# Second layer's wide blocks: the product with w_in by one level of Strassen's scheme over pairs of packets

## The chip, the cores and the metric

The kernel runs on one core of a Trainium2 chip. The metric is the device time of one execution in microseconds. A core has a matrix engine (TensorE, PE), whose weight loads are listed apart (PEld), and three engines for elementwise work: VectorE (DVE), ScalarE (ACT) and GpSimd (POOL). Each engine works through its own instructions in a fixed order, and instructions wait for each other across engines by semaphores. Data lie in SBUF, 128 partitions wide; matmuls write to PSUM, of which this kernel uses eight banks of 512 fp32 columns.

## The reference

Forgetting attention is followed by two MLPs. The second MLP, the only part that changes, is `_moe2_ref`; its x is the first MLP's output.

```python
def _moe2_ref(x, w_in, w_out, alpha):          # x 2304x512, w_in 512x2048, w_out 2048x512
    h = x @ w_in
    g = np.maximum(h, 0.0) + alpha * np.minimum(h, 0.0)
    return (g @ w_out).astype(np.float32)
```

## The kernel before, in words

The time axis has two layers of MLP blocks. Layer 0 works on blocks of 256 tokens while the attention of later tokens runs beside it on the other engines. Layer 1 is the second MLP: one narrow block of 256 tokens (t = 0) and four wide blocks of 512 tokens (`SIZES[1]`). The 2048 hidden units are cut into 16 packets of 128 (`NF`); a packet holds 128 columns of w_in and 128 rows of w_out.

Products have fp32 accuracy by splitting: `split` makes a high part (a cast by ScalarE to float32r) and a low part (the difference, by VectorE unless told otherwise) of each operand, and three matmuls, high by high, high by low and low by high, stand for one product. `packet(1, f)` keeps both parts of a packet's weights in SBUF for the whole of layer 1.

For one block, `mlp_block` returns `up`, `down` and `finish`. `up(f)` multiplies packet f's columns of w_in with the block's x: four chunks of 128 input features by three terms, 12 matmuls of 512 columns in one bank (L712). ScalarE makes the two relus of the result (L731, L735), VectorE joins them to the leaky relu `r` (L736), and `split` writes its high and low part into `ring`, a buffer for four packets. `down(f, g)` adds packet f's part of the output: four groups of 128 tokens by three terms, again 12 matmuls of 512 columns, in four banks that collect over all 16 packets (L758). `finish` scales the banks into `res` tiles and writes them out (L783, L785, L795). The main loop calls `up` three packets ahead of `down` (`LAG[1]` = 3), and `inputs` of the next block at f = 10.

`wide_inputs` loads x of a wide block from `x2_d` (an intermediate in DRAM), and splits it; the parts of consecutive blocks lie in two sets of tiles, so that a block's x is split while the one before is still in use. The order of each engine's instructions is made by a scheduler from the program's order and its own estimates; at run time it is fixed.

Of the kernel before, what the change touches and what calls it, by code (L numbers as in the profile page):

```python
# [19 lines left out]
def tile_forget_attention__then__two_mlps(  # L20
# [20 lines left out]
    nc = tc.nc  # L41
# [20 lines left out]
    REBASE, W_SCALE = 2.0**-111, 2.0**8  # L62
# [10 lines left out]
    ps = ctx.enter_context(tc.tile_pool(name="ps", bufs=2, space=PSUM))  # L73
# [11 lines left out]
    gate_s, gate_b, bsum, nalpha = misc[:, 0:1], misc[:, 1:2], misc[:, 4 : 4 + NCC], misc[:, 8 : 8 + NF]  # L85
# [167 lines left out]
    xf = {}  # L253
# [366 lines left out]
    x2_d = dram.tile([NB, P, NCC * T], F32, name="x2_d")  # L620


    SIZES = [[(t, 1) for t in range(NB - 2)] + [(NB - 2, 2)], [(0, 1)] + [(t, 2) for t in range(1, NB, 2)]]
    BLOCKS = [(layer, t) for layer in range(2) for t in range(len(SIZES[layer]))]

    def inputs(layer, t):

        first, count = SIZES[layer][t]
        if count == 2:
            return wide_inputs(layer, t, first)  # L630
# [16 lines left out]
        for c in range(NCC):  # L647
            on_pool = layer == 0 and t
            split(xh[c], xl[c], src[:, c], nc.gpsimd if on_pool else nc.vector)
        return xh, xl  # L650

    def wide_inputs(layer, t, first):
        xh, xl = [], []
        src = []
        for half in range(2):
            if layer == 1:
                src.append(xfp.tile([P, 2, 2, T], F32, tag="xf", name=f"x2_{t}_{half}"))
                for z in range(2):
                    nc.sync.dma_start(
                        out=src[half][:, :, z],  # L660
                        in_=x2_d[first + z, :, half * 2 * T : (half + 1) * 2 * T].rearrange("p (c n) -> p c n", n=T),
                    )
            for parts, tag, spare in ((xh, "xh", "raw"), (xl, "xl", "probs")):
                name = f"{tag}{layer}_{t}_{half}"
                if layer == 0:
                    if half:
                        part = two.tile([P, 1024], F32R, tag="raw", name=name)
                    else:
                        part = one.tile([P, 1024], F32R, tag=f"{tag}1", name=name)
                elif t % 2:  # L670
                    part = two.tile([P, 1088 if spare == "probs" else 1024], F32R, tag=spare, name=name)
# [15 lines left out]
    wide_ring = []  # L687

    def mlp_block(layer, t, x):


        xh, xl = x
        acc = acc_tiles(f"acc{layer}_{t}")
        banks = [a.rearrange("p a n -> p (a n)") for a in acc]
        first, count = SIZES[layer][t]
        TB = count * T
# [4 lines left out]
        def up(f):  # L701
# [37 lines left out]
            split(gh, gl, r, nc.gpsimd if layer == 0 and count == 1 else nc.vector)  # L739
            return gh, gl  # L740

        def down(f, g):
            w = packet(layer, f)
            if layer == 0:
                terms = ((w[2], g[0]), (w[3], g[0]), (w[2], g[1]))
                for d in range(NCC):
                    for n, (a, b) in enumerate(terms):
                        nc.tensor.matmul(  # L748
                            banks[d] if count == 2 else acc[d // 2][:, d % 2], a[:, d * P : (d + 1) * P], b,
                            start=(f == 0 and (d % 2 == 0 or count == 2) and n == 0),  # L750
                            stop=(f == NF - 1), skip_group_check=True,
                        )
            else:
                gh, gl = g
                _, _, woh, wol = w
                for m in range(TB // P):
                    for a, b in ((gh, woh), (gh, wol), (gl, woh)):
                        nc.tensor.matmul(  # L758
                            banks[m], a[:, m * P : (m + 1) * P], b,
                            start=(f == 0 and b is woh and a is gh), stop=(f == NF - 1 and a is gl),  # L760
                        )

        def finish():
            for m, bank in enumerate(banks):
                if m % 2 == 0:
                    pool = xfp if m else one
                    both = pool.tile([P, 1024], F32, tag="xf" if m else "res", name=f"res{layer}_{t}_{m}")
                res = both[:, m % 2 * 512 : (m % 2 + 1) * 512]
# [125 lines left out]
```

## Time and profile before

| what | value |
|---|---|
| time, median of 3 runs | 1048.67 us (1044.5 to 1049.79) |
| profiled execution, its own time | 1046.88 us |
| its span, first to last instruction | 1045.1 us |
| mean granted clock of TensorE | 0.996 of full speed |
| TensorE (PE) busy | 1030.9 us, 99% |
| ScalarE (ACT) busy | 625.7 us, 60% |
| VectorE (DVE) busy | 587.1 us, 56% |
| GpSimd (POOL) busy | 362.5 us, 35% |

The four wide blocks take the time from about 687 us to the end. A busy share is an average over the whole span; what an engine does in one stage is read from the table by stretches. Matmuls overlap in the pipeline, so the time from one start to the next, and not a matmul's duration, tells what it costs.

### The profile page before, as it was taken

What the parts mean: (1) busy time and instruction counts of PE and PEld (TensorE: products, weight loads), DVE (VectorE), ACT (ScalarE), POOL (GpSimd) and SP (SyncE); (2) the same over time, 40 slices, a digit from 0 to 9 for tenths busy, and PEclk for the clock granted to TensorE, in tenths of its full rate; (3) what the DMA queues carried; (4) which work ended last, traced back from release to release, by engine and by line L of the source; (5) the groups of instructions that cost most, each with busy time, mean ns of one, the idle gap of its engine ahead of it and who ended that gap; (6) DMA issues with size and microseconds to landing.
All of it is one profiled execution on the core that took longest, in us unless ns stands there. A gap on an engine that the chain in (4) does not pass through costs nothing.

```text
span 1045.1 us, 18431 instructions
## 1 busy us (share of the span) xinstructions
PE 1030.9 (99%) x6372; PEld 910.0 (87%) x6376; DVE 587.1 (56%) x1421; ACT 625.7 (60%) x1493; POOL 362.5 (35%) x768
## 2 busy tenths in 40 slices
PE   9899999999999999999999999999999999999998
PEld 4578899999999999999998888988888888888887
DVE  6979864787667775767665766532223224223222
ACT  5877876777778786878776766533234334333232
POOL 5656775666677566777550000000000000000000
PEclk9999999999999999999999999999999999999999
DMA  7988442343133341324115753200002002001001
GB/s 155 266 218 234 124 73 64 74 99 75 40 85 76 89 83 41 89 62 97 54 58 175 242 161 94 88 21 1 1 1 81 1 1 81 1 0 41 1 1 41
DMA packets 173470, 83.36 MB, mean 80 GB/s; under 512 B 135552, under 2 KB 160896, under 8 KB 173376
## 3 DMA queue, kind: packets, MB, share of 16 engines
q1 hardware_dynamic: 169296, 81.61, 29.8%
q10 hardware_dynamic: 4080, 0.57, 0.3%
q8 instruction: 50, 0.82, 0.3%
q14 instruction: 44, 0.36, 0.1%
HBM read 72.63 MB, written 9.51 MB: 79 GB/s over the span
## 4 chain that ended last, share of the span: by engine, by line
PE 85%; DMA 4%; ACT 3%; DVE 3%; POOL 2%; issue 1%; SPq 1%; ACTq 0%; DVEq 0%; POOLq 0%
PE hp L712 36%; PE acc L758 19%; PE acc L748 17%; PE av L527 4%; PE pt L511 4%; PE sc L456 2%; DMA wo<-in_moe_w_out_dram 2%; PE sc L455 1%; DMA vn<-in_v_dram 1%; DVE wt L142 1%; PE colsum L241 1%; PE sc L453 1%; DVE probs L431 1%; ACT probs L469 1%; SPq L332 1%
## 5 line engine op out<-in xcount | busy, mean ns | idle before, releaser
L712 PE MATMUL hp<-xh,w 128*128 128x256 f32 (+1 forms) x1536 | 396.5, 330 | 0.3 <-ACT r L731 0.3
L712 PEld LDWEIGHTS hp<-xh,w 128*128 128x128 f32 x1536 | 267.5, 189 | 26.9 <-ACT r L731 0.7
L712 PE MATMUL hp<-xl,w 128*128 128x256 f32 (+1 forms) x768 | 253.0, 329 | 0.0
L731 ACT ACTIVATE r<-hp 128x256 f32<-128x256 f32 (+1 forms) x208 | 96.3, 463 | 224.2 <-PE hp L712 214.9
L758 PE MATMUL acc<-w,ring 128*128 128x512 f32 x864 | 209.0, 390 | 0.0
L758 PEld LDWEIGHTS acc<-w,ring 128*128 128x128 f32 x864 | 161.3, 188 | 33.2
L748 PE MATMUL acc<-gh,w 128*128 128x256 f32 x896 | 172.3, 286 | 0.4 <-ACT res L774 0.3
L736 DVE SCALAR_TENSOR_TENSOR r<-u,misc,r 128x512 f32<-128x512 f32 (+1 forms) x80 | 55.8, 697 | 200.4 <-ACT u L735 200.4
L712 PEld LDWEIGHTS hp<-xl,w 128*128 128x128 f32 x768 | 145.2, 189 | 13.4 <-issue 0.4
L748 PEld LDWEIGHTS acc<-gh,w 128*128 128x128 f32 x896 | 136.0, 189 | 3.1 <-issue 1.6
L748 PE MATMUL acc<-gl,w 128*128 128x256 f32 x448 | 118.7, 288 | 1.8 <-POOL gl L131 1.8
L469 ACT ACTIVATE probs<-probs,nm 64x64 f32<-64x64 f32 (+4 forms) x160 | 90.0, 563 | 37.1 <-DVE nm L457 25.0
L480 POOL TENSOR_SCALAR probs<-probs,sm 64x64 f32<-64x64 f32 (+4 forms) x160 | 90.9, 581 | 60.5 <-DVE sm L477 49.9
L131 POOL TENSOR_TENSOR gl<-r,gh 128x256 fp32r<-128x256 f32 x112 | 89.5, 799 | 51.0 <-ACT gh L130 44.5
L131 DVE TENSOR_TENSOR ring<-r,ring 128x512 fp32r<-128x512 f32 (+1 forms) x96 | 62.1, 647 | 60.6 <-ACT ring L130 60.4
L457 DVE CUSTOM_DVE_ANT_0 probs<-sc,probs 128x320 f32<-128x320 f32 (+3 forms) x160 | 68.2, 427 | 41.0 <-PE sc L456 32.0
L130 ACT CAST ring<-r 128x512 fp32r<-128x512 f32 (+1 forms) x96 | 56.1, 584 | 53.3 <-DVE r L736 52.6
L748 PEld LDWEIGHTS acc<-gl,w 128*128 128x128 f32 x448 | 80.1, 188 | 4.6 <-POOL gl L131 2.5
L511 PE MATMUL pt<-ident,probs 128*128 128x128 f32 x480 | 74.4, 276 | 4.8 <-POOL probs L480 4.6
L545 DVE TENSOR_TENSOR xf<-av,xf 64x128 f32<-64x128 f32 (+3 forms) x88 | 28.0, 319 | 67.9 <-ACT xf L544 67.5
L511 PEld LDWEIGHTS pt<-ident,probs 128*128 128x128 f32 x480 | 54.7, 140 | 10.9 <-POOL probs L480 7.0
L431 DVE TENSOR_SCALAR probs<-cum,cumT 64x64 f32<-64x64 f32 (+4 forms) x137 | 62.5, 504 | 2.9 <-issue 0.9
(117 smaller groups left out, 1579.3 us busy)
## 6 DMA issues: line engine op xcount, KB each, us to landing
wi<-in_moe_w_in_dram SPq DMA_DIRECT2D x32, 512.0 KB, 4.9
wo<-in_moe_w_out_dram SPq DMA_DIRECT2D x32, 512.0 KB, 5.0
cum<-cum_d SPq DMA_DIRECT2D x32, 288.0 KB, 3.7
cum<-cum_d SPq DMA_DIRECT2D x30, 160.0 KB, 3.1
nat<-in_k_dram SPq DMA_DIRECT2D x64, 72.0 KB, 2.5
x_d<-res SPq DMA_DIRECT2D x18, 256.0 KB, 2.3
out_dram<-res SPq DMA_DIRECT2D x18, 256.0 KB, 2.1
vn<-in_v_dram SPq DMA_DIRECT2D x32, 128.0 KB, 2.8
```

The costliest lines, as they stand in the source:

```text
L130: nc.scalar.copy(hi, src)
L131: lo_eng.tensor_tensor(out=lo, in0=src, in1=hi.bitcast(F32), op=ALU.subtract)
L431: nc.vector.tensor_scalar(out=pt[:rows, :i1], in0=u.cums[h][:rows, :i1], scalar1=cumT[:rows, r, head : head + 1], scalar2=0.0, op0=ALU.sub ...
L457: nc.vector.tensor_tensor_reduce(out=pt[:rows, j0:j1], in0=scr, in1=pt[:rows, j0:j1], scale=SCALE if flip else -SCALE, scalar=init, op0=AL ...
L469: nc.scalar.activation(pt[:rows, :n], pt[:rows, :n], AF.Exp, bias=nm[:rows, m : m + 1], scale=1.0 if flip else -1.0, accum_out=sm[:rows, m ...
L480: nc.gpsimd.tensor_scalar(out=probs[r][:rows, :n], in0=probs[r][:rows, :n], scalar1=sm[:rows, m : m + 1], scalar2=1.0, op0=ALU.mult, op1=A ...
L511: nc.tensor.transpose(tp[:, o : o + P], u.probs[h][r][:, k0 : k0 + P], ident)
L712: nc.tensor.matmul(hs, a[:, c], b[c], start=(n == 0), stop=(n == len(terms) * NCC - 1))
L731: relus.append(nc.scalar.activation(r, hs, AF.Relu, scale=1.0 / W_SCALE).ins)
L736: nc.vector.scalar_tensor_tensor(out=r, in0=u, scalar=nalpha[:, f : f + 1], in1=r, op0=ALU.mult, op1=ALU.add)
L748: nc.tensor.matmul(banks[d] if count == 2 else acc[d // 2][:, d % 2], a[:, d * P : (d + 1) * P], b, start=(f == 0 and (d % 2 == 0 or count ...
L758: nc.tensor.matmul(banks[m], a[:, m * P : (m + 1) * P], b, start=(f == 0 and b is woh and a is gh), stop=(f == NF - 1 and a is gl),)
```

## The change

In the wide blocks of layer 1, two packets (256 hidden units) are taken together. Their weights form a matrix of 2 by 2 blocks: the packet (1 or 2) by the half of the input features (`halves`: chunks 0 and 1, or 2 and 3). The block's x forms another one: the half of the features by the half of the tokens (256 each). One level of Strassen's scheme (in the form of Winograd, which shares sums) replaces the eight block products by seven. Each product is six matmuls of 256 columns, two chunks by three terms.

- `strassen_inputs` replaces `wide_inputs` for layer 1. It loads x in two pieces, forms four differences (`t1` to `t4`) on VectorE and GpSimd, and splits seven operands, numbered by product in `OPERANDS`. The tiles are one set: the next block's operands are written into the same ones.
- `weight_sums(pair, which)` forms four sums of weight blocks from high and low parts: sums 1, 2 and 4 on GpSimd (three, two and two steps of 256 columns), sum 3 on VectorE (three steps), and splits them into `sums`, one tile of high and one of low parts. `next_sums` calls it a pair ahead.
- `up_first(f)`, for the first packet of a pair, issues products 1, 6 and 5 into banks a, b and c. ScalarE copies a and c to `t1` and `t5`, VectorE makes `u2` = b + `t1`. `up_second(f)` adds product 7 to b, 2 to a, 3 to c and 4 to b. Before 4, VectorE reads b for `u3`; after it, b for `cc`, of which GpSimd makes the second half from `u3` and `t5`. Two leaky relus (`relu_pair`, `prelu`) give both packets.
- `finish` of the wide blocks takes its `res` tiles from the tags `ph` and `pl`.

```diff
-    def wide_inputs(layer, t, first):
+    def strassen_inputs(t, first):
+        src = []
+        for j in range(2):
+            src.append(xfp.tile([P, 2, 2 * T], F32, tag="xf", name=f"x2_{t}_{j}"))
+            nc.sync.dma_start(out=src[j], in_=x2_d[first + j].rearrange("p (k n) -> p k n", k=2))
...
+        t3 = minus(room[:, : 2 * T], b22, b12, nc.gpsimd)
+        t1 = minus(b12, b12, b11, nc.vector)
+        t2 = minus(room[:, 2 * T :], b22, t1, nc.vector)
+        for c in range(2):
+            cols = slice(c * T, (c + 1) * T)
+            minus(t4[c], b21[:, cols], t2[:, cols], nc.gpsimd)
+        for n, x in ((1, b11), (6, t2), (5, t1), (7, t3), (2, b21), (3, b22)):
+            split(*parts[n], x)
...
+    def weight_sums(pair, which):
...
+        if 1 in which:
+            chain(nc.gpsimd, s[1], h2[:, 0], (add, h2[:, 1]), (add, l2[:, 0]), (add, l2[:, 1]))
+            chain(nc.gpsimd, s[2], s[1], (sub, h1[:, 0]), (sub, l1[:, 0]))
+            sums[2:] = [s[2]]
+        else:
+            chain(nc.vector, s[3], h1[:, 0], (sub, h2[:, 0]), (add, l1[:, 0]), (sub, l2[:, 0]))
+            chain(nc.gpsimd, s[4], h1[:, 1], (sub, sums[2]), (add, l1[:, 1]))
+        for n in which:
+            split(sums[0][:, n - 1], sums[1][:, n - 1], s[n])
...
+        def multiply(bank, n, a, start):
+            (ah, al), (bh, bl) = a, x[0][n]
+            for c in range(2):
+                for z, (lhs, rhs) in enumerate(((ah, bh), (ah, bl), (al, bh))):
+                    nc.tensor.matmul(
+                        bank, lhs[:, c * P : (c + 1) * P], rhs[:, c],
...
+        def up_first(f):
...
+            multiply(a, 1, left[1], True)
+            nc.scalar.copy(t1, a)
+            multiply(b, 6, left[6], True)
+            nc.vector.tensor_tensor(out=u2, in0=b, in1=t1, op=ALU.add)
+            multiply(c, 5, left[5], True)
+            nc.scalar.copy(t5, c)
...
+            next_sums(f, (1, 2))
+            return holder
+
+        def up_second(f):
...
+            multiply(b, 7, left[7], False)
+            nc.vector.tensor_tensor(out=u3, in0=b, in1=t1, op=ALU.add)
+            multiply(a, 2, left[2], False)
+            relu_pair(r[:, :T], u[:, :T], a)
+            multiply(c, 3, left[3], False)
+            nc.vector.tensor_tensor(out=u2, in0=c, in1=u2, op=ALU.add)
+            relu_pair(r[:, T:], u[:, T:], u2)
+            holder.extend(prelu(r, u, f - 1))
+            multiply(b, 4, left[4], False)
+            cc = one.tile([P, 512], F32, tag="vn", name=f"cc_{name}")
+            nc.gpsimd.tensor_tensor(out=cc[:, T:], in0=u3, in1=t5, op=ALU.add)
+            nc.vector.tensor_tensor(out=cc[:, :T], in0=b, in1=t1, op=ALU.add)
...
+            relu_pair(r, u, cc)
+            g = prelu(r, u, f)
+            next_sums(f, (3, 4))
+            return g
...
-        return up, down, finish
+        return up_strassen if layer == 1 and count == 2 else up, down, finish
```

How the order of instructions changes, on VectorE first, in the second wide block of layer 1 around packets 9 to 11. Before, a packet takes two instructions, the leaky relu (L736) and the low part for `ring` (L131):

```order
L736 SCALAR_TENSOR_TENSOR r_2_9_11302<-u_2_9_11303,misc,r_2_9_11302 128x512
L131 TENSOR_TENSOR ring_9986<-r_2_9_11302,ring_9982 128x512
L736 SCALAR_TENSOR_TENSOR r_2_10_11334<-u_2_10_11335,misc,r_2_10_11334 128x512
L131 TENSOR_TENSOR ring_9987<-r_2_10_11334,ring_9983 128x512
L736 SCALAR_TENSOR_TENSOR r_2_11_11384<-u_2_11_11385,misc,r_2_11_11384 128x512
L131 TENSOR_TENSOR ring_9988<-r_2_11_11384,ring_9984 128x512
```

After the change, at the same place, from the leaky relu of packet 9 (L812) to the first half of `cc` of packet 11. `sum_6_12123`, `sum_6_12227` and `sum_6_12228` are sums 1, 3 and 4 for packets 12 and 13, `sum_7_12346` is sum 3 for packets 14 and 15, `u_2_11` is `u3`, `u_2_10` is `u2`:

```order
L812 SCALAR_TENSOR_TENSOR ph_2_9_12066<-pl_2_9_12067,misc,ph_2_9_12066 128x512
L131 TENSOR_TENSOR sums_l<-sum_6_12123,sums_h 128x256
L131 TENSOR_TENSOR ring_9986<-ph_2_9_12066,ring_9982 128x512
L850 TENSOR_TENSOR u_2_11_12183<-p_2_10_12097,t_2_10_12099 128x256
L131 TENSOR_TENSOR sums_l<-sum_6_12227,sums_h 128x256
L854 TENSOR_TENSOR u_2_10_12101<-p_2_10_12098,u_2_10_12101 128x256
L812 SCALAR_TENSOR_TENSOR ph_2_11_12181<-pl_2_11_12182,misc,ph_2_11_12181 128x512
L131 TENSOR_TENSOR sums_l<-sum_6_12228,sums_h 128x256
L723 TENSOR_TENSOR sum_7_12346<-w_14_60_10032,w_15_16_10094 128x256
L131 TENSOR_TENSOR ring_9987<-ph_2_11_12181,ring_9983 128x512
L723 TENSOR_TENSOR sum_7_12346<-sum_7_12346,w_14_59_10033 128x256
L860 TENSOR_TENSOR cc_11_12217<-p_2_10_12097,t_2_10_12099 128x256
```

Between the two leaky relus of neighbouring packets there are now low parts of weight sums and reads of banks, and `cc` stands last.

On GpSimd, before, the last work is the low part of a hidden packet of layer 0's last narrow block; then its program ends:

```order
L131 TENSOR_TENSOR gl_6_13_9093<-r_13_9094,gh_6_13_9092 128x256
L131 TENSOR_TENSOR gl_6_14_9125<-r_14_9126,gh_6_14_9124 128x256
L131 TENSOR_TENSOR gl_6_15_9157<-r_15_9158,gh_6_15_9156 128x256
L889 UNCONDITIONAL_BRANCH
L889 ISA
```

After the change it goes on through the wide blocks. This is its part of the place shown for VectorE: sum 1 for packets 14 and 15 (three steps), the second half of `cc` of packet 11, sum 4 for packets 12 and 13, and sum 2 for packets 14 and 15:

```order
L723 TENSOR_TENSOR sum_7_12277<-w_15_16_10094 128x256
L723 TENSOR_TENSOR sum_7_12277<-sum_7_12277,w_15_15_10095 128x256 x2
L859 TENSOR_TENSOR cc_11_12217<-u_2_11_12183,t_2_10_12100 128x256
L723 TENSOR_TENSOR sum_6_12228<-w_12_48_9900,sum_6_12124 128x256
L723 TENSOR_TENSOR sum_6_12228<-sum_6_12228,w_12_47_9901 128x256
L723 TENSOR_TENSOR sum_7_12278<-sum_7_12277,w_14_60_10032 128x256
L723 TENSOR_TENSOR sum_7_12278<-sum_7_12278,w_14_59_10033 128x256
```

Eight operations a pair have come to GpSimd. Its first step of sum 1 waits for VectorE's low part of the sum 1 before, since one tile holds that sum; its `cc` waits for VectorE's `u3`; sum 4 shares a tile with sum 3 and waits for the low part of that.

## Rows read from the trace of the kernel before

**Rows 1.** The page: span, and busy time of each engine.

```profile
span 1045.1 us, 18431 instructions
PE 1030.9 (99%) x6372; PEld 910.0 (87%) x6376; DVE 587.1 (56%) x1421; ACT 625.7 (60%) x1493; POOL 362.5 (35%) x768
```

**Rows 2.** The table by stretches: layer 0, then a wide block.

```profile
core 0: us, PE busy (x) PEld busy (x) DVE busy (x) ACT busy (x) POOL busy (x), PEclk, DMA share, GB/s
300.00:400.00 100.00, 100.00 (x836) 99.79 (x836) 71.35 (x208) 79.00 (x213) 68.19 (x142) 1.00 0.35 76
800.00:900.00 100.00, 100.00 (x442) 82.61 (x441) 29.65 (x42) 33.98 (x61) 0.00 (x0) 1.00 0.07 22
```

**Rows 3.** Groups of instructions from 640 us on, shapes apart.

```profile
L736 DVE SCALAR_TENSOR_TENSOR r<-u,misc,r 128x512 f32<-128x512 f32 x64 | 48.1, 751 | 188.5 <-ACT u L735 188.5
L131 DVE TENSOR_TENSOR ring<-r,ring 128x512 fp32r<-128x512 f32 x65 | 45.1, 693 | 43.8 <-ACT ring L130 43.8
L130 ACT CAST ring<-r 128x512 fp32r<-128x512 f32 x65 | 40.3, 620 | 47.9 <-DVE r L736 47.5
L731 ACT ACTIVATE r<-hp 128x512 f32<-128x512 f32 x64 | 38.2, 597 | 173.9 <-PE hp L712 173.9
L131 DVE TENSOR_TENSOR ring<-r,ring 128x256 fp32r<-128x256 f32 x16 | 6.8, 423 | 4.5 <-ACT ring L130 4.5
L130 ACT CAST ring<-r 128x256 fp32r<-128x256 f32 x16 | 6.5, 404 | 5.2 <-DVE r L736 5.2
```

**Rows 4.** TensorE's timeline (start, duration, what, count): narrow block, then the last wide.

```profile
669.35 0.52 PE L712 MATMUL hp<-xr,w 128*128 128x256 f32 x3
669.71 1.56 PE L758 MATMUL acc<-w,ring 128*128 128x512 f32 x6
671.11 0.28 PE L712 MATMUL hp<-xgh,w 128*128 128x256 f32 x1
...
1024.98 2.88 PE L758 MATMUL acc<-w,ring 128*128 128x512 f32 x12
1027.70 0.39 PE L712 MATMUL hp<-xh,w 128*128 128x512 f32 x1
1030.42 11.04 PE L758 MATMUL acc<-w,ring 128*128 128x512 f32 x48
```

**Rows 5.** Timeline: one packet's way from ScalarE to VectorE and back.

```profile
704.03 0.59 ACT L735 ACTIVATE u<-hp 128x512 f32<-128x512 f32 x1
704.65 0.75 DVE L736 SCALAR_TENSOR_TENSOR r<-u,misc,r 128x512 f32<-128x512 f32 x1 [1.88 <-ACT u L735]
705.44 0.62 ACT L130 CAST ring<-r 128x512 fp32r<-128x512 f32 x1 [0.82 <-DVE r L736]
```

**Rows 6.** Timeline: VectorE and GpSimd in the attention stage.

```profile
127.08 0.73 POOL L131 TENSOR_TENSOR gl<-r,gh 128x256 fp32r<-128x256 f32 x1
127.12 1.24 DVE L131 TENSOR_TENSOR w<-wt,w 128x512 fp32r<-128x512 f32 x1 [1.88 <-POOL sm L409]
127.77 1.19 POOL L131 TENSOR_TENSOR xl<-xf,xh 128x256 fp32r<-128x256 f32 x1
...
228.28 0.73 POOL L131 TENSOR_TENSOR gl<-r,gh 128x256 fp32r<-128x256 f32 x1 [0.66 <-ACT gh L130]
228.31 0.98 DVE L395 TENSOR_TENSOR ql<-turned,xs 64x256 fp32r<-64x256 f32 x1
```

**Rows 7.** Lines L131 and L142: count, then ns min/median/max; L142 from 560 us.

```profile
L131 POOL TENSOR_TENSOR gl<-r,gh x112: 721/737/1210, 66.6 to 559.8; 128x256 fp32r<-128x256 f32 x112
...
L142 DVE SCALAR_TENSOR_TENSOR wt<-wo,wt x15: 682/691/693, 562.7 to 654.1; 128x512 uint32<-128x512 uint32 x15
```

**Rows 8.** Groups from 100 to 560 us that read 256 columns of PSUM.

```profile
L545 DVE TENSOR_TENSOR xf<-av,xf 64x256 f32<-64x256 f32 x16 | 6.7, 421 | 14.1 <-ACT xf L544 14.0
...
L544 ACT COPY xf<-av 64x256 f32<-64x256 f32 x16 | 5.9, 367 | 1.8 <-DVE xf L545 0.7 <-PE av L527 0.7
```

**Rows 9.** Timeline: the last result of the last block.

```profile
1041.50 0.60 ACT L783 ACTIVATE res<-acc 128x512 f32<-128x512 f32 x1 [0.76 <-PE acc L758]
```

More of the change, by code (lines that the diff above doesn't have):

```diff
@@ L629, in inputs @@
         if count == 2:
-            return wide_inputs(layer, t, first)
+            return wide_inputs(t, first) if layer == 0 else strassen_inputs(t, first)
         if layer == 0:
@@ L650, in inputs, with wide_inputs @@
         return xh, xl
-    def wide_inputs(layer, t, first):
+    def wide_inputs(t, first):
         xh, xl = [], []
-        src = []
         for half in range(2):
[L656 to L671, printed above, removed]
+            for parts, tag in ((xh, "xh"), (xl, "xl")):
+                name = f"{tag}0_{t}_{half}"
+                if half:
+                    part = two.tile([P, 1024], F32R, tag="raw", name=name)
                 else:
-                    part = one.tile([P, 1024], F32R, tag=f"{tag}{half}", name=name)
+                    part = one.tile([P, 1024], F32R, tag=f"{tag}1", name=name)
                 parts += [part[:, c * 2 * T : (c + 1) * 2 * T] for c in range(2)]
-        if layer == 0:
-            src = [xf.pop(first + z) for z in range(2)]
+        src = [xf.pop(first + z) for z in range(2)]
         for c in range(NCC):
-            if layer == 1:
-                split(xh[c], xl[c], src[c // 2][:, c % 2].rearrange("p z n -> p (z n)"))
-                continue
             for z in range(2):
@@ L684, in wide_inputs, with minus @@
         return xh, xl
-    ring, relus = [], []
-    wide_ring = []
+    OPERANDS = {
+        1: (one, "xh0", 1024), 6: (one, "xl0", 1024), 5: (two, "raw", 1024), 2: (one, "xh1", 1024),
+        7: (two, "raw", 1024), 3: (two, "probs", 1088), 4: (two, "probs", 1088),
+    }
+    def strassen_inputs(t, first):
[3 more added lines that the diff above has]
+            nc.sync.dma_start(out=src[j], in_=x2_d[first + j].rearrange("p (k n) -> p k n", k=2))
+        parts = {}
+        for n, (pool, tag, cols) in OPERANDS.items():
+            both = pool.tile([P, cols], F32R, tag=tag, name=f"xs{t}_{n}")
+            parts[n] = [both[:, z * 2 * T : (z + 1) * 2 * T] for z in range(2)]
+        (b11, b21), (b12, b22) = ([x[:, k] for k in range(2)] for x in src)
+        def minus(out, a, b, eng):
+            eng.tensor_tensor(out=out, in0=a, in1=b, op=ALU.subtract)
+            return out
+        room = one.tile([P, 1024], F32, tag="res", name=f"t_{t}")
+        t4 = [two.tile([P, T], F32, tag="r", name=f"t4_{t}_{c}") for c in range(2)]
+        t3 = minus(room[:, : 2 * T], b22, b12, nc.gpsimd)
[7 more added lines that the diff above has]
+        for c in range(2):
+            split(*(x[:, c * T : (c + 1) * T] for x in parts[4]), t4[c])
+        if not sums:
+            weight_sums(0, (1, 2))
+            weight_sums(0, (3, 4))
+        return {n: [x.rearrange("p (c n) -> p c n", c=2) for x in pair] for n, pair in parts.items()}, None
@@ new lines, in tile_forget_attention__then__two_mlps, with halves, chain @@
+    ring, relus = [], []
+    wide_ring, sums = [], []
+    def halves(f):
+        return [x.rearrange("p (k n) -> p k n", k=2) for x in (y.rearrange("p c n -> p (c n)") for y in packet(1, f)[:2])]
+    def weight_sums(pair, which):
+        if not sums:
+            sums.append(xfp.tile([P, 4, 2 * P], F32R, tag="xf", name="sums_h"))
+            sums.append(one.tile([P, 4, 2 * P], F32R, tag="xl1", name="sums_l"))
+        (h1, l1), (h2, l2) = halves(2 * pair), halves(2 * pair + 1)
+        f32 = lambda x: x.bitcast(F32)
+        def chain(eng, out, first, *rest):
+            for n, (op, x) in enumerate(rest):
+                eng.tensor_tensor(out=out, in0=out if n else f32(first), in1=f32(x), op=op)
+        add, sub = ALU.add, ALU.subtract
+        s = {
+            n: one.tile([P, 2 * P], F32, tag=("ql00", "ql10", "ql11", "ql11")[n - 1], name=f"sum{n}_{pair}")
+            for n in which
+        }
+        if 1 in which:
[7 more added lines that the diff above has]
+            split(sums[0][:, n - 1], sums[1][:, n - 1], s[n])
@@ L740, in up, with next_sums @@
             return gh, gl
+        pair_state = {}
+        def multiply(bank, n, a, start):
+            (ah, al), (bh, bl) = a, x[0][n]
+            for c in range(2):
+                for z, (lhs, rhs) in enumerate(((ah, bh), (ah, bl), (al, bh))):
+                    nc.tensor.matmul(
+                        bank, lhs[:, c * P : (c + 1) * P], rhs[:, c],
+                        start=(start and c == 0 and z == 0), stop=(c == 1 and z == 2), skip_group_check=True,
+                    )
+        def next_sums(f, which):
+            if f // 2 + 1 < NF // 2 or t + 1 < len(SIZES[1]):
+                weight_sums((f // 2 + 1) % (NF // 2), which)
@@ new lines, in temp, with prelu, relu_pair @@
+        def temp(tag, name, bufs):
+            return two.tile([P, T], F32, tag=tag, name=name, bufs=bufs)
+        def prelu(r, u, f):
+            nc.vector.scalar_tensor_tensor(
+                out=r, in0=u, scalar=nalpha[:, f : f + 1], in1=r, op0=ALU.mult, op1=ALU.add
+            )
+            gh, gl = (y[f % 4][:, :TB] for y in ring)
+            split(gh, gl, r)
+            return gh, gl
+        def relu_pair(r, u, src):
+            nc.scalar.activation(r, src, AF.Relu, scale=1.0 / W_SCALE)
+            nc.scalar.activation(u, src, AF.Relu, scale=-1.0 / W_SCALE)
@@ new lines, in up_second @@
+        def up_second(f):
+            name = f"{t}_{f}"
+            left, (a, b, c), (t1, t5, u2), holder = pair_state.pop(f // 2)
+            r, u = (two.tile([P, 512], F32, tag=tag, name=f"{tag}1_{name}") for tag in ("ph", "pl"))
+            u3 = temp("gl", f"u3_{name}", 3)
+            multiply(b, 7, left[7], False)
[10 more added lines that the diff above has]
+            nc.vector.tensor_tensor(out=cc[:, :T], in0=b, in1=t1, op=ALU.add)
+            r, u = (two.tile([P, 512], F32, tag=tag, name=f"{tag}2_{name}") for tag in ("ph", "pl"))
+            relu_pair(r, u, cc)
+            g = prelu(r, u, f)
+            next_sums(f, (3, 4))
+            return g
@@ L764, in finish @@
             for m, bank in enumerate(banks):
[L765 to L768, printed above, removed]
+                if layer == 1 and count == 2:
+                    res = two.tile([P, 512], F32, tag=("ph", "pl")[m % 2], name=f"res1_{t}_{m}")
+                else:
+                    if m % 2 == 0:
+                        pool = xfp if m else one
+                        both = pool.tile([P, 1024], F32, tag="xf" if m else "res", name=f"res{layer}_{t}_{m}")
+                    res = both[:, m % 2 * 512 : (m % 2 + 1) * 512]
                 if layer == 0:
```

11 lines of the change are left out of this document (added).

## The prediction

> **What bounds the kernel now.** I read the page's busy times first. TensorE is busy 99% of a span of 1045.1 us [rows 1]; the profiled execution itself took 1046.9 us, that is 1.8 us around the span. Then I read the table by stretches, because the change touches only the last third: in a stretch of 100 us of the wide blocks TensorE is busy in all 100 us, its granted clock is 1.00 (2.4 GHz), VectorE works 30 us, ScalarE 34 us and GpSimd nothing at all [rows 2]. So TensorE alone sets the time there, and every column that it doesn't stream is a gain, as long as the other engines keep up. The timeline of TensorE gives its pace: 12 matmuls of 512 columns take 2.72 us (1024.98 to 1027.70, and again to 1030.42), and three of 256 columns take 0.36 us up to the 512s that follow, 0.12 us each [rows 4]. Six 512s followed by a 256 take 1.40 us where six at 2.72/12 = 0.227 us would take 1.36, so a turn from 512 to 256 columns costs 0.04 us [rows 4].
>
> **TensorE's part of the change.** A pair of packets goes up in 24 matmuls of 512 columns and down in 24: 4 x 2.72 = 10.88 us. After it, up is seven products of six matmuls of 256 columns, 42 x 0.12 = 5.04 us; down stays 5.44; about three turns from 512 to 256 cost 0.13. That is 10.6 us, a gain of 0.28 us a pair and 9.0 us over 32 pairs (four blocks of eight). An eighth of the columns is gone, but each matmul costs 0.013 us beyond its columns (0.12 against 256/2.4 GHz = 0.107) and there are 42 for 24. The 42 weight loads don't show: in the first layer, where nearly everything is 256 wide, they are busy 99.8% and TensorE still 100% [rows 2].
>
> **What the other engines get.** Durations: on VectorE a two-tile operation takes 0.75 (the PReLU step) or 0.69 us at 512 columns and 0.42 at 256; a ScalarE cast takes 0.62 and 0.40, a relu of 512 from PSUM 0.60 [rows 3]; a VectorE add that reads PSUM takes 0.42 and a ScalarE copy from PSUM 0.37 at 256 columns [rows 8]. A GpSimd subtraction of 256 columns takes 0.72 at least, 0.74 in the median [rows 7]. From one engine to the next some 0.04 us pass (704.62 to 704.65, 705.40 to 705.44) [rows 5]. A pair now needs of VectorE four adds with PSUM (1.7), two PReLU steps (1.5), two low parts of 512 (1.4), three steps of sum 3 (1.3) and four low parts of sums (1.7): 7.6 us. ScalarE: two copies, two relus of 256 from PSUM, two from SBUF, two relus of 512, two casts of 512, four of 256: 6.4. GpSimd: seven steps of sums and one add of outputs, 8 x 0.74 = 5.9. Each is below 10.6, so by busy time alone all of it lies beside TensorE.
>
> **What speaks against that: VectorE and GpSimd stop each other.** In the attention stage GpSimd starts a subtraction at 127.08 and ends at 127.81; VectorE's, whose two inputs both lie in SBUF, starts at 127.12 and ends at 128.36, 0.55 us after GpSimd's end. GpSimd's next starts at 127.77 and ends at 128.96, 0.60 after VectorE's. With 256 columns VectorE ends 0.28 after GpSimd (228.28 + 0.73 = 229.01; 228.31 + 0.98 = 229.29) [rows 6]. The same kind of VectorE operation takes 0.69 where GpSimd is still [rows 7]. So the two behave as if they shared a port of SBUF (so I call it below): the later one waits and then needs 0.60 (GpSimd, 256), 0.55 or 0.28 (VectorE, 512 and 256). The Trainium skill, "SBUF — State Buffer", section "Who interferes with whom", states this as a rule: a VectorE instruction with two SBUF inputs and a GpSimd instruction that reads SBUF share one port pair, and the second to start is blocked until the first ends. Rows and rule agree on who blocks whom; by the rule the pair is held for a whole instruction, and what the sum would be by that stands as rival 3. The rows show a shorter hold: the one that waited ends 0.14 us earlier than a free one would. By the rows a pair needs 8 x 0.60 + 4 x 0.55 + 7 x 0.28 = 9.0 us of the port, under TensorE's 10.6. Nothing is lost to mere throughput, but latencies grow, and VectorE, ScalarE and GpSimd work in a fixed order in which each waits for the others.
>
> **The loop through that order.** In the order of pair 10/11 (shown with the change) VectorE's add `cc` for one pair stands behind the low part of sum 4 and two steps of the next sum 3, sum 4 waits on GpSimd behind its half of `cc` and three steps of sum 1, and sum 1 waits for VectorE's low part of the sum 1 before, which stands behind the PReLU step that waits for the last `cc`. From the end of one `cc` (0): two relus to 1.28 (SBUF source, taken as 0.62 each), PReLU step 1.32 to 2.07, low of sum 1 to 2.49, GpSimd's first step 2.53 to 3.27. VectorE asks at 2.77 with a packet's low part, gets the port at 3.27 and ends at 3.82; second step to 4.42; the add `u3` reads PSUM beside it to 4.24; low of sum 3 to 4.70; third step to 5.30; `u2` to 5.12; two relus of 256 to 5.96; GpSimd's `cc` 5.34 to 6.08; PReLU step to 6.68 (0.60, 0.05 over a blocked 0.55 as 0.75 is over 0.69); sum 4 to 7.28 and 8.06; cast to 8.50; low of sum 4 asks at 8.54, waits for GpSimd's sum 2 until 8.84, ends 9.12; sum 2's second step to 9.72; step of sum 3 to 10.00, low part to 10.65, step to 11.07, and the next `cc` ends at 11.5. Without the port the same sum is 1.32 + 0.75 + 0.42 + 0.04 + 6 x 0.78 + 0.44 + 0.04 + 0.42 + 0.46 + 0.69 + 0.42 + 0.42 = 10.1. So the loop lies between 10.1 and 11.5 us. In pair 12/13 the low part of sum 1 stands ahead of the PReLU step, and the same walk gives 11.25. I take 11.4, near the upper end, because the rows show the blocking each time that the two meet.
>
> TensorE doesn't feel a late `cc` at once. Product 7 of the next pair waits for `u2`, which stands behind `cc`: allowed some 1.1 us after product 4's end, while TensorE itself comes there after 0.48 + 0.72 + 2.72 + 0.72 + 0.45 = 5.1 us. So 4.0 us of lateness are free, once, and then each pair costs what the loop does.
>
> **At the three seams** between wide blocks VectorE gets seven low parts of 512 columns, two differences of inputs and two results, 11 x 0.69 = 7.6 us more; before, its eight low parts fell into a stage where it was idle 70% [rows 2]. In the walk VectorE waits 3.0 us of a pair for other engines, so a part goes there; following the same order through pair 14/15 I come to 14.5 instead of 11.4. I take 3 us a seam, bounds 0 and 7.6. The inputs of the first wide block and the first sums lie beside the narrow block, on a GpSimd that is idle, ahead of use: nothing. x2 comes in two loads a block for four, on a queue that moves 22 GB/s there [rows 2]: nothing. The end: before, the last result starts at 1041.50, its three companions staggered ahead of it [rows 9]; now the last four matmuls end all four banks together, so two results queue behind the first two: 0.7, bounds 0 and 1.5.
>
> **Sum.** 32 x (11.4 - 10.88) = +16.6; free lateness -4.0; seams 3 x 3 = +9; end +0.7: +22.3 on the profiled execution's 1046.9, so 1069 us. That execution is 1.8 us below the median of 1048.67 and within the runs' 1044.5 to 1049.8.
>
> **Rivals.**
> 1. TensorE stays the bound: the loop is at most 10.6 us, because GpSimd and VectorE meet less often than I walked. For it speaks the sum without the port, 10.1, and the port's 9.0 us a pair; against it that 19 operations a pair need the port, and the rows of blocking. Time: 1046.9 - 9.0 + 0.7 + about 1.5 at seams = 1040.
> 2. The loop comes out at 10.6 to 11.0, and what TensorE saves is given back: with 10.85 and 3 us a seam, less the free lateness, 1046.9 - 1.0 + 9 - 4 + 0.7 = 1052. It needs about half of the meetings in the walk.
> 3. The port is held for whole instructions. Then a pair needs 5.9 + 1.5 + 1.4 + 1.3 + 1.7 = 11.8 us of it, which is a bound whatever the order, and the seams' 7.6 us come on top: 32 x 0.92 = +29.4, +22.8, -4, +0.7: 1096. Against it stand the rows, where a waiting operation ends 0.14 us earlier than a free one would. The Trainium skill's page "SBUF — State Buffer" words it so in the section named above: whichever starts first keeps the port for its whole instruction.
> That the change doesn't do what it says is excluded by the order: each pair has its 42 matmuls of 256 columns.
>
> **Chances.** Forecast (loop 11.0 to 11.8, 1057 to 1085) 0.55; rival 1 0.20; rival 2 (1043 to 1056) 0.15; rival 3 and worse 0.10. The range takes in rival 1's 1040 and a little beyond the forecast's upper edge: 1039 to 1088. A difference under 0.5% (5.2 us) can't be told from none. Faster by more: rival 1 and the lower edge of rival 2, 0.22; within: most of rival 2, 0.10; slower: 0.68.
>
> **What the profile after would show.** If I am right, TensorE in the wide blocks falls under 95% busy, its waits there name VectorE's `u2` or `u3` or ScalarE's copies, a pair takes about 11.4 us, GpSimd's steps average over 0.80 us or VectorE's 256-column low parts over 0.45, and VectorE has few idle stretches. If TensorE shows no idle time and a pair takes 10.6, rival 1 holds and my walk put too many meetings on the port. If VectorE's and GpSimd's busy times of a pair add to more than the pair although both are dense, it is rival 3. If a 256-column matmul takes other than 0.12 us apart, the TensorE sum is wrong whatever the rest.

## The result and the profile after

The changed kernel takes 1059.51 us (median of four runs, 1057.28 to 1061.22) against 1049.18 us before on the same chip: a ratio of 1.0107, 95% interval 1.0072 to 1.0142. A second timing on another chip gave 1.0108 (1.0072 to 1.0144). So it is slower, by 10.3 us where +20 on the median was forecast.

The page of the changed kernel, to be held against [rows 1]:

```profile
span 1057.8 us, 20572 instructions
PE 1026.7 (97%) x6948; PEld 925.6 (88%) x6952; DVE 777.7 (74%) x1797; ACT 700.0 (66%) x1765; POOL 604.7 (57%) x1036
```

TensorE is busy 4.2 us less than before in a span that is 12.7 us longer: it now waits. Where it waits, the table by stretches of the same kernel says (columns as in [rows 2]):

```profile
core 0: us, PE busy (x) PEld busy (x) DVE busy (x) ACT busy (x) POOL busy (x), PEclk, DMA share, GB/s
800.00:900.00 100.00, 94.38 (x575) 82.28 (x574) 83.52 (x144) 53.39 (x134) 65.61 (x72) 1.00 0.07 23
...
800.00:850.00 50.00, 48.60 (x300) 42.87 (x299) 37.89 (x70) 25.55 (x66) 31.94 (x37) 1.00 0.01 3
857.00:883.00 26.00, 22.24 (x132) 18.63 (x131) 25.14 (x40) 14.65 (x36) 17.52 (x19) 1.00 0.12 41
```

Over 100 us TensorE is busy 94% (100% before, [rows 2]). Within them, 800 to 850 is the middle of a block, TensorE at 97%, and 857 to 883 the seam to the next block: TensorE 86%, VectorE 25.1 of 26 us. The timeline of TensorE at that seam shows the waits one by one (start, length, in brackets the idle time ahead and who ended it):

```profile
875.83 0.87 PE L799 MATMUL p<-xs,w 128*128 128x256 f32 x6
876.97 0.50 PE L799 MATMUL p<-xs,sums_h 128*128 128x256 f32 x2 [0.27 <-ACT pl L821]
878.54 0.97 PE L799 MATMUL p<-xs,w 128*128 128x256 f32 x6 [1.07 <-DVE u L850]
881.72 0.50 PE L799 MATMUL p<-xs,sums_h 128*128 128x256 f32 x2 [1.72 <-DVE u L854]
```

`u3` (L850) and `u2` (L854) are the two adds that the prediction named. Over all wide blocks TensorE's waits name the same two most (us in total, times, longest; L835 is the first of the two adds that make `u2`, L837 the copy of bank c):

```profile
PE p L799 <- DVE u L850: 3.9, 3, 1.8
PE p L799 <- DVE u L854: 3.4, 2, 1.7
PE p L799 <- DVE u L835: 2.8, 5, 0.6
PE p L799 <- ACT t L837: 1.6, 4, 0.4
```

VectorE's timeline over the stretch at the seam shows why they are late:

```profile
875.79 1.22 DVE L687 TENSOR_TENSOR x<-x,x 128x512 f32<-128x512 f32 x1
876.93 1.22 DVE L812 SCALAR_TENSOR_TENSOR ph<-pl,misc,ph 128x512 f32<-128x512 f32 x1
878.07 0.41 DVE L850 TENSOR_TENSOR u<-p,t 128x256 f32<-128x256 f32 x1
878.41 0.61 DVE L131 TENSOR_TENSOR sums_l<-sum,sums_h 128x256 fp32r<-128x256 f32 x1
878.94 1.26 DVE L687 TENSOR_TENSOR t<-x 128x512 f32<-128x512 f32 x1
880.12 1.21 DVE L131 TENSOR_TENSOR ring<-ph,ring 128x512 fp32r<-128x512 f32 x1
881.25 0.41 DVE L854 TENSOR_TENSOR u<-p,u 128x256 f32<-128x256 f32 x1
```

No gap lies between these rows. The two differences of inputs (L687), a PReLU step and a low part take 1.2 us each, where such operations took 0.69 to 0.75 [rows 3], and `u2` stands behind all four. The groups of VectorE and GpSimd over the wide blocks (mean ns behind the comma):

```profile
L131 DVE TENSOR_TENSOR sums_l<-sum,sums_h 128x256 fp32r<-128x256 f32 x124 | 65.7, 539 | 33.5 <-ACT sums_h L130 33.5
L131 DVE TENSOR_TENSOR ring<-ph,ring 128x512 fp32r<-128x512 f32 x64 | 58.4, 912 | 10.6 <-ACT ring L130 10.3
L812 DVE SCALAR_TENSOR_TENSOR ph<-pl,misc,ph 128x512 f32<-128x512 f32 x64 | 55.8, 872 | 24.2 <-ACT pl L821 24.2
L854 DVE TENSOR_TENSOR u<-p,u 128x256 f32<-128x256 f32 x32 | 13.2, 412 | 0.0
L723 POOL TENSOR_TENSOR sum<-sum,w 128x256 f32<-128x256 f32 x151 | 133.3, 891 | 8.7
L723 POOL TENSOR_TENSOR sum<-w 128x256 f32<-128x256 f32 x30 | 29.6, 987 | 89.0 <-DVE sums_l L131 89.0
L723 POOL TENSOR_TENSOR sum<-w,sum 128x256 f32<-128x256 f32 x31 | 29.3, 944 | 1.8 <-DVE sums_l L131 1.8
```

VectorE's operations with two SBUF inputs are stretched (0.54, 0.91, 0.87 for 0.42, 0.69, 0.75 [rows 3]), GpSimd's steps too (0.89 to 0.99 for 0.74 [rows 7]); `u2`, which reads a bank, keeps its 0.41 [rows 8].

Pair by pair this reads as follows, worked out from TensorE's timeline: us from a pair's first product to the next pair's, for the eight pairs of wide block 2, and behind it TensorE's idle time in that block, counted as the start-to-start times beyond 0.227 us (512 columns) or 0.12 (256) where more than 0.1 is over. The experiments' rows are used below.

```
changed     12.67 15.06 10.40 10.53 11.99 10.63 10.51 10.49   idle 8.1
e_once      10.48 10.49 10.45 10.47 10.47 10.47 10.47 10.47   idle 0
e_memset3   10.52  9.13 11.91 10.45 10.48 10.49 10.49 10.49   idle 0
e_inputs    10.49 11.60  9.38 10.48 11.76 10.71 10.51 10.49   idle 1.5
e_turn      10.00 14.07  9.68 10.48 12.38 10.69 10.51 10.94   idle 4.7
e_turn_own  10.50 11.22 11.10 10.45 10.66 10.46 10.46 10.49   idle 1.4
```

The changed kernel doesn't lose 0.8 us in every pair. Five of the eight pairs run at 10.4 to 10.6, near TensorE's own 10.47, and 6.5 of the block's 8.1 idle us lie in the first three pairs behind the seam; the fifth pair has 1.5 more. Over the four blocks the idle time is 21.8 us, 16.3 of it in the first three pairs of blocks 2 to 4 (16.3 again in a second profile of the same kernel).

### The profile page after: what moved, and what is told of

Read it like the earlier page. It is cut to its first block, busy times and chain, and to the rows that moved or that the text cites. A ratio compares the mean times of both kernels' runs of the same rounds, so it can differ in the third digit from the quotient of the medians.

```text
span 1057.8 us, 20572 instructions
## 1 busy us (share of the span) xinstructions
PE 1026.7 (97%) x6948; PEld 925.6 (88%) x6952; DVE 777.7 (74%) x1797; ACT 700.0 (66%) x1765; POOL 604.7 (57%) x1036
## 3 DMA queue, kind: packets, MB, share of 16 engines
q1 hardware_dynamic: 166096, 81.61, 29.3%
## 4 chain that ended last, share of the span: by engine, by line
PE 59%; DVE 18%; POOL 9%; ACT 5%; issue 5%; DMA 3%; SPq 1%; ACTq 0%; POOLq 0%; DVEq 0%
PE hp L763 17%; PE acc L873 16%; PE acc L883 6%; POOL sum L723 6%; PE p L799 4%; PE av L527 4%; PE pt L511 4%; DVE sums_l L131 3%; DVE sum L723 3%; DVE ring L131 2%; DVE ph L812 2%; PE sc L456 2%; PE sc L453 1%; DMA vn<-in_v_dram 1%; DVE xs L131 1%
## 5 line engine op out<-in xcount | busy, mean ns | idle before, releaser
L763 PE MATMUL hp<-xh,w 128*128 128x256 f32 (+1 forms) x1024 | 229.1, 301 | 0.5 <-ACT r L782 0.5
L763 PEld LDWEIGHTS hp<-xh,w 128*128 128x128 f32 x1024 | 171.5, 190 | 6.6 <-ACT r L782 1.0
L763 PE MATMUL hp<-xl,w 128*128 128x256 f32 (+1 forms) x512 | 152.6, 298 | 0.0
L723 POOL TENSOR_TENSOR sum<-sum,w 128x256 f32<-128x256 f32 x160 | 141.7, 894 | 10.4 <-DVE w L131 1.2
L131 POOL TENSOR_TENSOR gl<-r,gh 128x256 fp32r<-128x256 f32 x112 | 89.4, 798 | 51.8 <-ACT gh L130 44.6
L799 PE MATMUL p<-xs,sums_h 128*128 128x256 f32 x512 | 98.5, 285 | 8.7 <-DVE u L854 3.4
L799 PEld LDWEIGHTS p<-xs,sums_h 128*128 128x128 f32 x512 | 80.5, 189 | 16.6 <-DVE u L835 6.3
L130 ACT CAST sums_h<-sum 128x256 fp32r<-128x256 f32 x128 | 49.8, 404 | 66.7 <-POOL sum L723 57.9
L131 DVE TENSOR_TENSOR sums_l<-sum,sums_h 128x256 fp32r<-128x256 f32 x128 | 68.4, 543 | 33.5 <-ACT sums_h L130 33.5
L799 PE MATMUL p<-xs,w 128*128 128x256 f32 x576 | 85.4, 283 | 4.0 <-DVE u L850 3.9
L799 PEld LDWEIGHTS p<-xs,w 128*128 128x128 f32 x576 | 79.6, 189 | 10.3 <-DVE u L850 4.8
```

Source lines behind the costliest of these rows:

```text
L723: eng.tensor_tensor(out=out, in0=out if n else f32(first), in1=f32(x), op=op)
L763: nc.tensor.matmul(hs, a[:, c], b[c], start=(n == 0), stop=(n == len(terms) * NCC - 1))
L799: nc.tensor.matmul(bank, lhs[:, c * P : (c + 1) * P], rhs[:, c], start=(start and c == 0 and z == 0), stop=(c == 1 and z == 2), skip_group ...
```

## The experiments

The stage named here is the time from TensorE's first wide product to its last matmul: 353.3 us before (688.15 to 1041.46), 362.8 changed.

**No sums after the first pair.**
```
-            if f // 2 + 1 < NF // 2 or t + 1 < len(SIZES[1]):
+            if False:
```


> Leaves out the weight sums of every pair but the first: all pairs multiply with the sums of packets 0 and 1; the products, the adds of outputs and the seams stay. Theory (what makes TensorE wait is the loop that the sums make through VectorE, ScalarE and GpSimd): TensorE's 21.8 us of waits in the wide blocks nearly vanish, a pair takes TensorE's own 10.5 us, and the time is 1059.6 - 21.8 + 0 to 8 for seams = 1038 to 1046. Rival (the seven products with their adds u2, u3, cc and the relus are a loop of their own that is longer than 10.5): over 1052 although the sums are gone.

1035.29 us, ratio to before 0.9896 (0.9877 to 0.9916), somewhat under the theory's span. In its table by stretches TensorE has no idle time:

```profile
800.00:900.00 100.00, 100.00 (x634) 90.78 (x633) 50.34 (x88) 46.81 (x106) 10.55 (x12) 1.00 0.06 22
```

A pair takes 10.47 us and the stage 339.3. The products, their adds and even the seams' inputs don't hold TensorE; the sums must be there too. This also measures TensorE's own gain: 353.3 - 339.3 = 14.0 us. But without the sums GpSimd has next to nothing to do (11 us in 100), so this run can't tell the sums' waits from GpSimd's reading; the next two can.

**GpSimd's steps of the sums write but read nothing**: two fills of the tile for each step, and in a second kernel three (`range(3)`):
```
-                eng.tensor_tensor(out=out, in0=out if n else f32(first), in1=f32(x), op=op)
+                if eng is nc.gpsimd:
+                    for z in range(2):
+                        eng.memset(out, 0.25 * n)
...
```


> GpSimd's steps of sums 1, 2 and 4 read nothing: each step is two fills of the same tile instead of one add (the values of the sums are left out), with the same waits on the tile; two fills are to take about 0.7 us together, an estimate from the fills of other widths in the trace. Theory (VectorE and GpSimd stop each other when both read SBUF): VectorE's 256-column low parts go back from a mean of 0.54 to 0.42-0.45 and its 512 ones from 0.91 to 0.69-0.72, a pair in the middle of a block from 10.96 to 10.5, and the time to 1040 to 1048. Rival (the fixed order and the tiles that hold one sum each set the loop, whether or not the instructions are stretched): 1054 or more.

> As the run with two fills for each GpSimd step of the sums (whose fills took 0.313 us each, 0.63 a step, against 0.74 for an add that runs alone), but three fills a step: 0.94 us, longer than the add alone and as long as the adds took on average in the changed kernel (0.91). Values of the sums are left out again. Theory (GpSimd's reads of SBUF stop VectorE): 1033 to 1038, as with two fills, and VectorE's low parts stay at 0.42 to 0.50 and 0.69 to 0.72. Rival (GpSimd's shorter steps made the gain there): the stalls come back, 1045 or more.

1034.00 us (0.9886, 0.9867 to 0.9905) with two fills, below the theory's 1040, and 1035.06 (0.9877, 0.9850 to 0.9903) with three; no idle time on TensorE in either. Groups of VectorE and GpSimd with three fills:

```profile
L131 DVE TENSOR_TENSOR sums_l<-sum,sums_h 128x256 fp32r<-128x256 f32 x124 | 53.5, 437 | 5.8 <-ACT sums_h L130 5.7
L131 DVE TENSOR_TENSOR ring<-ph,ring 128x512 fp32r<-128x512 f32 x64 | 44.0, 688 | 16.4 <-ACT ring L130 16.1
L854 DVE TENSOR_TENSOR u<-p,t 128x256 f32<-128x256 f32 x32 | 13.5, 423 | 34.0 <-PE p L803 34.0
L725 POOL MEMSET sum<- 128x256 f32 x636 | 183.0, 312 | 83.1 <-DVE sums_l L131 65.9
```

GpSimd is busy nearly as long as with the adds (183 us for 133.3 + 29.6 + 29.3 = 192), it still waits for VectorE's low parts, and VectorE does the same work; the reads of the steps are gone, and with them all of the loss. VectorE's low parts are back at 0.44 and 0.69, and `u3` (L854 here) now waits 34 us for TensorE, 3.4 in the changed kernel. So GpSimd's reading is the cause: the same work on VectorE and the same shared tiles cost TensorE nothing without it. The order isn't wholly the same, since a fill doesn't read the step before it and the scheduler orders each kernel anew: in the middle of a block GpSimd does sum 2 ahead of `cc` with two fills, where it stood behind sum 4. No run holds the order fixed and takes away the reads alone; but the orders of the runs below, which keep the reads, all leave TensorE 4.7 us or more of idle time, and the stretched operations in the rows above show the blocking directly. The Trainium skill, "SBUF — State Buffer", section "Who interferes with whom", says that a VectorE instruction with two SBUF inputs contends with a GpSimd one that reads SBUF and not with one that only writes; these runs agree, on both halves.

**The seams without their inputs**: blocks 2 to 4 multiply block 1's operands, so loads, differences, casts and low parts fall away.
```
+        if built:
+            return built[0], None
...
```


> Wide blocks 2 to 4 multiply the operands of the first wide block again: the loads, differences, casts and low parts of inputs at the three seams are left out. Theory (the seams cost TensorE 4.3 us each beyond the 10.96 of a pair): 1059.6 - 13 = 1046 to 1050. Rival (the lateness is the loop's and is only shown at the seams): 1055 to 1060.

1041.65 us (0.9954, 0.9939 to 0.9969), below the theory's 1046: the inputs of blocks 2 to 4 cost 1059.5 - 1041.65 = 17.9 us, some 6 a block (18.0 by the stages). TensorE has no idle time at the seam between blocks 1 and 2, which here lies at 768 (columns as in [rows 2]):

```profile
765.00:785.00 20.00, 20.00 (x129) 18.12 (x129) 15.34 (x30) 11.09 (x29) 12.82 (x16) 1.00 0.00 1
```

Of the 16.3 us of idle time in the first three pairs of blocks 2 to 4, 0.8 are left. Another 2.3 fall away in block 1: its third pair idles 2.2 us in the changed kernel, because the scheduler put the first differences of block 2's inputs there already. The stage is 344.8, that is 5.5 us above the run without sums. I take those 5.5 for the loop; 4.7 are idle time, most of it in the fifth pairs.

**Tiles of their own for the sums** of pairs 1, 3 and 5 and for sum 4:
```
+        if pair in (1, 3, 5):
+            if 1 in which:
+                rooms[pair] = one.tile([P, 4, 2 * P], F32, tag="res", name=f"sums_{pair}")
+            s = {n: rooms[pair][:, n - 1] for n in which}
...
```


> The sums of pairs 1, 3 and 5 get a tile of their own each (room that lies idle between seams), and sum 4 of the others no longer shares sum 3's; nothing is left out. Theory (GpSimd's first step of sum 1 and of sum 4 wait for VectorE's low part of the sum that was in the tile before, and this closes the loop): GpSimd's waits on the low parts fall from 91 us by over half, pairs 1 to 6 of a block come to 10.5 to 10.7, and the time to 1048 to 1053. Rival (the engines have no time left: what the two take from each other fills the pair): 1057 to 1062, with GpSimd's waits only moved.

The theory missed and the rival came: 1062.01 us (1.0155, 1.0131 to 1.0178), stage 362.9. GpSimd waits less for low parts of sums, 36 us for 91, but 37 us before `cc`, behind a cast of ScalarE. The middle of a block did get better: no idle time from the fourth pair on, not even the fifth pair's 1.5. But the first pair behind each seam now idles 3.9 to 4.6 us where it idled 1.7 to 2.1. The shared tiles set where the loss shows, not how large it is.

**The turned order.** Blocks 2 and 4 take the pairs from 7 down to 0, so that the last pair's sums serve the next block's first pair. Then the same with sum 4's own tile, and with all own tiles (pairs at positions 1, 3 and 5):
```
+        def turn(f):
+            return NF - 2 - f + 2 * (f % 2) if layer == 1 and count == 2 and t % 2 == 0 else f
...
```


> Wide blocks 2 and 4 take the pairs of packets in the opposite order, 7 to 0, so that the last pair of one block is the first of the next and its sums stand already: three of 32 sets of sums fall away, all three at the seams; nothing else changes. Theory (the stalls come from the seams, where VectorE has inputs, results and sums at once and each is stretched by GpSimd's reads): of 17 us at the three seams 10 to 15 go, 1044 to 1050. Rival (the loop of 10.98 us in the middle of a block feeds the lateness that shows at the seams): 1053 to 1058, the three sets' own share of TensorE's waits (3/32 of 21.8 = 2 us) and a little more.

> The run with turned pair order, and sum 4 has a tile of its own, so that VectorE's first step of the next sum 3 needs not wait for the low part of sum 4 (VectorE waits 1.9 us for that sum in the middle of a block). Theory: the loop comes from 10.98 to about 10.2, lateness shrinks from pair to pair instead of growing, and stalls of 3 to 6 us go beside the turned order's: 1038 to 1045. Rival (work that starts earlier meets GpSimd's reads more often): within 2 us of the turned order alone.

> As before it, with sum 4's own tile, and all four sums of the pairs at positions 1, 3 and 5 of a block in a tile that lies idle between seams. Theory (tiles hold up GpSimd): 1036 to 1044, below or equal to sum 4's own tile alone. Rival (GpSimd that runs ahead only meets VectorE at other places, as the own tiles without the turned order did: 1062): at or above the run with sum 4's tile alone.

1048.83 us (1.0015, 1.0003 to 1.0028), 1047.89 (0.9999, 0.9985 to 1.0012) and 1042.44 (0.9947, 0.9930 to 0.9965). Three of 32 sets of sums, taken away at the seams, gave back 9 to 10 us (8.7 in the stage: 354.1 for 362.8; 1.0015 for 1.0107), where an even share would be about 2. At the seams 10.9 of 16.3 us of idle time went, the theory's 10 to 15; 2.7 came back in the other pairs. Sum 4's own tile alone adds nothing that can be told; the rival's "within 2 us" holds. With all own tiles the stage is 346.5 (348.3 in a second profile): tiles that were worth nothing while the sums stood in the seams are worth about 6 us once they don't. VectorE's busy time in the last one's 800 to 900 us is high, and TensorE is not held up by it:

```profile
800.00:900.00 100.00, 98.93 (x620) 88.86 (x619) 91.15 (x149) 56.61 (x142) 64.56 (x70) 1.00 0.06 22
```

**All results of blocks 1 to 3 on ScalarE**, on top of that:
```
-                elif m % 2:
+                elif m % 2 or (count == 2 and t + 1 < len(SIZES[1])):
```


> The run with turned order and the sums' own tiles, and in wide blocks 1 to 3 ScalarE reads out all four result banks (two of them before, VectorE the other two). Theory (what is left of the stalls, 6.6 us, is VectorE's list at the seams): VectorE sheds 2 x 0.68 us at each seam, and of the 3.7 us of stalls in blocks 2 to 4 one to three go: 1039 to 1041.5. Rival (four results in a row on ScalarE free the banks later than two beside two, and the next block's first products with w_out wait for them): 1043 to 1047.

1044.06 us (0.9970, 0.9952 to 0.9989), stage 347.0, idle time 7.3 us for 6.6: nothing gained. VectorE's 0.68 us at each of two results is not what the pairs behind the seam wait for.

**The best version and the changed kernel once more**, on one chip:

> The turned order with the sums' own tiles once more, with more rounds and beside the changed kernel on one chip. Theory: it beats the kernel before, with the whole interval of the ratio below 1 (0.993 to 0.997 before). Rival: the gain was chance, and the interval holds 1.

> The changed kernel itself, unaltered, beside the one above: ratio 1.007 to 1.014 to the kernel before if its slowdown is the same on another chip; a ratio below 1.005 would put part of the slowdown down to the chip of the first timing.

1043.73 us (0.9956, 0.9933 to 0.9980) and 1059.67 (1.0108, 1.0072 to 1.0144). The turned order with own tiles beats the kernel before by about 0.5% and the change as it was made by 1.5%.

## Why the prediction was right in direction and wrong in its parts

The mechanism was right: VectorE and GpSimd stop each other, TensorE waits for `u2` and `u3`, and that costs more than the saved columns. The terms of the sum were not: the loop was forecast 16 us too large, the seams 9 and TensorE's gain 5 too small. Part of the direction is luck: with the loop and the gain as measured and the seams as forecast the sum would be -14.0 + 5.5 + 9 + 0.7 = +1.2, no slowdown at all. From the stage's start to the end of the span +10.8 us were measured (stage +9.5, end +1.3).

- **TensorE's own work: -9.0 forecast, -14.0 measured** (run without sums). The old pace held too: the stage before is 32 x 10.88 and 5.1 of other work. A pair now takes 10.47 and not 10.6. The timeline of TensorE in the changed kernel has 18 matmuls of 256 columns between the starts of the first two of these rows and 12 of 512 columns between those of the last two:

```profile
843.58 0.39 PE L799 MATMUL p<-xs,sums_h 128*128 128x256 f32 x2
...
845.70 2.93 PE L883 MATMUL acc<-w,ring 128*128 128x512 f32 x12
848.47 0.88 PE L799 MATMUL p<-xs,w 128*128 128x256 f32 x6
```

  2.12/18 = 0.118 us and 2.77/12 = 0.231. In the run without sums, where nothing waits, the means are 0.119 and 0.228 from start to start, and 42 x 0.119 + 24 x 0.228 = 10.47. The 0.04 us that the prediction charged for a turn from 512 to 256 columns aren't there: a 512 ahead of a 256 takes 0.228 in that run as any other, and pairs with two turns and with four take 10.47 alike. In the narrow block of [rows 4] all 512s are slower, 0.233, with a 256 behind them or not. The turns' 0.13 a pair are 4 of the 5 us; the stage's other work is 0.8 shorter (339.3 - 32 x 10.47 = 4.3).
- **The loop: +16.6 - 4.0 over the old pace, that is 32 x (11.4 - 10.6) - 4.0 = +21.6 over TensorE's new one, forecast; +5.5 measured** (run without the seams' inputs). This is the step that failed: "each pair costs what the loop does". The walk itself was good. VectorE's timeline of the pair that was walked:

```profile
837.43 0.41 DVE L723 TENSOR_TENSOR sum<-sum,w 128x256 f32<-128x256 f32 x1
837.76 0.41 DVE L860 TENSOR_TENSOR cc<-p,t 128x256 f32<-128x256 f32 x1
...
839.40 0.75 DVE L812 SCALAR_TENSOR_TENSOR ph<-pl,misc,ph 128x512 f32<-128x512 f32 x1 [0.23 <-ACT pl L821]
...
840.84 1.01 DVE L131 TENSOR_TENSOR ring<-ph,ring 128x512 fp32r<-128x512 f32 x1 [0.35 <-ACT ring L130]
841.77 0.41 DVE L850 TENSOR_TENSOR u<-p,t 128x256 f32<-128x256 f32 x1
...
846.49 0.51 DVE L131 TENSOR_TENSOR sums_l<-sum,sums_h 128x256 fp32r<-128x256 f32 x1 [1.88 <-ACT sums_h L130]
847.02 0.85 DVE L723 TENSOR_TENSOR sum<-w,w 128x256 f32<-128x256 f32 x1
...
848.74 0.41 DVE L860 TENSOR_TENSOR cc<-p,t 128x256 f32<-128x256 f32 x1
```

  From the end of `cc` at 838.17 the PReLU step starts after 1.23 (walk 1.32), `u3` ends after 4.01 (4.24), the low part of sum 4 after 8.83 (9.12), and the next `cc` after 10.98 (11.5). The order of steps and every meeting are as walked; the half microsecond gathers step by step, chiefly because VectorE starts an operation some 0.07 us before the one ahead ends (837.43 + 0.41 = 837.84, and `cc` starts at 837.76), where the walk added whole durations. But one pair is not 32. In the run without the seams' inputs, 768.21 to 853.63 us hold eight pairs at 10.68: the order differs from pair to pair, the time from one `cc` to the next there is 10.1 to 11.6 us, and longer ones are made good by shorter ones within the free lateness. That is rival 2's loop (10.6 to 11.0).
- **The seams: +9 forecast (bounds 0 to 22.8 for three), +17.9 measured.** The prediction let the added work flow into VectorE's 3.0 us of waiting in one pair. In fact VectorE is filled for 25 us, the two added differences shown above take 1.2 us (1.04 and 1.05 on average over the seams, the low parts of inputs of 512 columns 0.78 and 0.95) and not 0.69, and `cc`'s lateness behind product 4, 4.8 to 5.7 us in the pairs before, rises to 8.0 in the last pair of the block: past what is free. The idle times of the first three pairs of blocks 2 to 4 add up to 6.5 + 6.2 + 3.6 = 16.3. It is inputs and sums together: without the inputs 0.8 of these are left, with the three sets of sums gone 5.4.
- **The end: +0.7 forecast, +1.3 measured**: last matmul to end of span 4.97 us for 3.63, within its bounds.
- The start, costed at nothing, came 1.9 us later in the profile shown (690.06 for 688.15), but at 687.98 in a second profile of the same kernel: it belongs to one execution, not to the change.

Sum: -14.0 + 5.5 + 17.9 + 1.3 = +10.7, against -9.0 + 21.6 + 9 + 0.7 = +22.3. The measured terms are steps from one run to the next (before, without sums, without the seams' inputs, whole), so they add up by construction; taken away in another order, the loop and the seams would share the loss otherwise. The signs that the prediction gave were met (TensorE 94% in 800 to 900 us, waits on `u2` and `u3`, GpSimd's steps over 0.80, low parts over 0.45), and a block of eight pairs did take 92.3 us (772.28 to 864.57), 11.5 a pair; but that average is made of 10.5 and 15, and an average could not tell the loop from the seam. Rival 1's pace, 10.5, is that of most pairs in the middle of a block, but not of all, as the fifth pair's 1.5 us show, and its 1040 us were not met; rival 2's 1052 fell short as well, by the seams; rival 3 is out, since it asks for 11.8 us in every pair and eight pairs without a seam's inputs take 10.68 each.

## What to carry to other kernels

A lateness in a side chain costs nothing until it passes what the bound engine can run ahead; so walk the place where extra work arrives (a seam) and the pairs behind it, and don't multiply the loop of one ordinary round by all rounds. Look for work that can be made not to arrive there: turning the order of every second block saved three of 32 sets of sums, and the kernel came level with the one before (1.0015 for 1.0107). And when an engine is brought in to help, ask whether it reads the same memory as the engine it helps: here 183 us of GpSimd's writing cost TensorE nothing, and 192 us of its reading cost over 20.

## What the runs showed of the hardware

- GpSimd's fills of SBUF (0.312 us for 256 columns) run beside VectorE's operations with two SBUF inputs without stretching them: 0.437 and 0.688 us, where beside GpSimd's adds they take 0.539 and 0.912 on average.
- VectorE's operations that follow each other without a wait overlap by some 0.07 us in the records, so a chain of them is shorter than the sum of its durations: most of the 0.5 us by which the walked loop came out shorter.
- 42 matmuls of 256 columns among 24 of 512 cost 10.47 us a pair in the run without sums, whether the width falls from 512 to 256 twice or four times in the pair: a change of width cost nothing that can be told there.
